# Other row orders for one scratch array, the residual rows and the output rows of a spectral filter with an MLP

## The chip, the cores and the metric

The kernel runs on one core of a Trainium2 chip. The metric is device time in microseconds (us). The time before is 407.89 us, the median of three runs (407.39 to 407.97). The profile is of one execution that took 407.44 us; its span, from the first to the last instruction, is 405.2 us, so 2.24 us lie around it. All times on the trace count from the start of the span.

## The reference

```python
def _A_ref(x, w_r, w_i):
    X = rfft2(x); X = X * (w_r + 1j * w_i)
    return irfft2(X, (S, D))
def _B_ref(x, w1, b1, w2):
    h = x @ w1 + b1
    return (h * tanh(softplus(h))) @ w2          # Mish
xn = _layernorm(A_x)
return A_x + _A_ref(xn, A_w_r, A_w_i) + _B_ref(xn, B_w1, B_b1, B_w2)
```

x has S = 2048 rows of D = 512 floats (4 MB), the MLP's hidden width is F = 1792. The result is the input plus a filter in the two-dimensional frequency domain plus an MLP, both of the normalized input.

## The kernel before, in words

Row number 1024 w + 16 t + 4 g + 2 i + q is written as w (2 halves), t (64), and the residue s2 = 4 g + 2 i + q of 16. The work is in **four groups g** of 512 rows.

**The MLP** runs as 56 tiles (g, f), f one of 14 slices of F, each with two half tiles. `mlp_up` does 12 matmuls `ph` (L735), a Mish on ScalarE (L743) and a split into two half-precision parts (L343 on ScalarE, L344 on VectorE); `mlp_down` does 12 matmuls `pa` (L88 to L92), some tiles later. After the last up tile of a group g < 3, `rows_back` (L778) loads the group's 512 residual rows into `macc[g]`, two transfers of 512 KB. After its last down tile `mlp_end` (L787) adds the MLP's sum to them (L793), and for g = 3 stores each quarter at once, one half from SyncE's queue (SP) and one from ScalarE's.

**The transform** takes four steps out (`s1_forward`, `p2_unit`, `d_pair`, and the product with the weights in `spectrum`) and four back. Between the steps the data is turned through scratch arrays in DRAM: `d_y1`, `d_a`, `d_t`. In `dp_unit` the tile `at` goes to `d_a` (L693); `ip_unit` loads it turned as `ai` (L701), multiplies (`psT`), and its tile `tt` goes to `d_t` (L717). `at`, `tt` and the earlier `y1` share three buffers, so a new one is written once the transfer of the third one before has landed. `spectrum` also moves a few short rows, `g<-es` (L609) and `u<-h` (L665), and uses the former in VectorE's L656. Two tiles `y` (L832) take the residual rows of the last group.

**The last step**, `s1_inverse`, runs eight times, for (g, q) in the order (3,0), (3,1), (0,0), (0,1), (1,0), (1,1), (2,0), (2,1). Each takes two tiles `yi` of 128 partitions (L843), made of two 64-partition halves, one for each of two parities. They come from the two planes of `d_t`, one transfer per half. Twelve matmuls `psY` (L866) follow, then VectorE (L882, L883) and GpSimd (L884) add the result to the residual rows; for g < 3 `store_rows` (L856) then sends 512 KB out in two transfers. In the loop over the eight, a step first loads the `yi` of the next one, then issues the stores of the one before, then multiplies.

**The order.** Loads and stores stand in SP's one instruction stream, in order; an issue that waits holds all behind it. TensorE's order in the last step is that of the program: half tiles of the MLP between the eight steps, as many as a rule with `T_LAG` and `T_HOLD` gives:

```python
while done[0] - start < T_LAG + k * (total - T_HOLD - T_LAG - start) / (n - 1) and half_tile():
    pass
```

With 15 half tiles left and n = 8, they stand 3, 1, 1, 2, 1, 1, 1, 1 ahead of the steps and 4 behind the last one.

Of the kernel before, what the change touches and what calls it, by code (L numbers as in the profile page):

```python
# [11 lines left out]
F16 = mybir.dt.float16  # L12
# [7 lines left out]
P = 128  # L20
NS2 = 16
# [6 lines left out]
E_UP = 11  # L28
N_WGT = 117.6
B_END = 97  # L30
T_LAG = 2.5
T_HOLD = 4


O_P2, O_IP2, O_D, O_ID2, O_ID = 0, 1024, 2048, 4096, 5120
# [4 lines left out]
def spectral_mlp_kernel(ctx, tc, x, wt, w0, w1, b1, w2, cT, cIT, cM, out):  # L40
    nc = tc.nc
# [11 lines left out]
    dp = ctx.enter_context(tc.tile_pool(name="dp", bufs=1, space=bass.MemoryType.DRAM))  # L53
# [1 line left out]
    nc.scalar.preload_act_table_set("mish")  # L55
    xv = x.rearrange("(p s) d -> p s d", s=NS2)

    xp = x.rearrange("(w t s) d -> t w s d", w=2, s=NS2)
    outp = out.rearrange("(w t s) d -> t w s d", w=2, s=NS2)


    d_y1 = dp.tile([64, P, 256], F16, tag="d_y1", name="d_y1")
    d_a = dp.tile([16, 2, P, 2 * 256], F16, tag="d_a", name="d_a")
    d_t = dp.tile([2, 64, 64, 256], F16, tag="d_t", name="d_t")

    @contextmanager
    def in_order(*engines):
# [18 lines left out]
    def mm3(ps, stat, mov, start, stop, order=False):  # L86

        first = nc.tensor.matmul(ps, stat(0), mov(0), start=start, stop=False)  # L88
        if order:
            tc.keep_in_program_order(first)  # L90
        nc.tensor.matmul(ps, stat(0), mov(1), start=False, stop=False)  # L91
        return nc.tensor.matmul(ps, stat(1), mov(0), start=False, stop=stop)  # L92
# [27 lines left out]
    def butterfly(out, a, b, scale, name):  # L120

        bc = tp.tile([P, 256], F32, tag="bc", name=f"bc_{name}", bufs=2)
        nc.scalar.mul(bc, b, scale)
        t = tp.tile([P, 4, 2, 64], F32, tag="bt", name=f"bt_{name}", bufs=2)
        av = a.rearrange("p (k e) -> p k e", k=4)
        bv = bc.rearrange("p (k e) -> p k e", k=4)
        nc.vector.scalar_tensor_tensor(t[:, :, 0], av, scale, bv, op0=ALU.mult, op1=ALU.add)
        last = nc.vector.scalar_tensor_tensor(t[:, :, 1], av, scale, bv, op0=ALU.mult, op1=ALU.subtract)  # L128
        tv = t.rearrange("p k c e -> p k (c e)")
        nc.scalar.copy(out[:, :, 0, :], tv)  # L130
        nc.gpsimd.tensor_sub(out[:, :, 1, :], tv, out[:, :, 0, :])  # L131
        return last.ins
# [565 lines left out]
    def ip_unit(c, g):  # L698
        fg = 4 * c + g
        ai = qp.tile([P, 4, 2, 2, 64], F16, tag="q1", name=f"ai_{fg}")  # L700
        nc.sync.dma_start(ai.rearrange("p (b r) h c e -> p b (r h c e)", b=2), d_a[fg].rearrange("b p e -> p b e"))  # L701
        ps = ps_f.tile([P, 2, 4, 64], F32, tag="f", name=f"psT_{fg}")
        for k in range(2):
            parts = [(1, slice(0, 1)), (0, slice(1, 4))] if fg == 0 else [(0, slice(0, 4))]
            for n, (v, ls) in enumerate(parts):
                mm3(
                    ps[:, k, ls],
                    lambda h: c_ip2[:, k, v, h, :],
                    lambda h: ai[:, ls, h, k, :],
                    True,  # L710
                    True,
                    k == 0 and n == 0,
                )
        tt = tp.tile([P, 4, 2, P], F16, tag="q2", name=f"tt_{fg}", bufs=3)
        butterfly(tt, ps[:, 0].rearrange("p l e -> p (l e)"), ps[:, 1].rearrange("p l e -> p (l e)"), 2.0**-12, f"t_{fg}")
        for be in range(2):
            nc.sync.dma_start(  # L717
                d_t[be].rearrange("a (c f) e -> (a c) (f e)", c=2)[:, fg * 512 : (fg + 1) * 512],
                tt[:, 2 * be : 2 * be + 2].rearrange("p l h e -> p (l h e)"),
            )  # L720


    macc, yacc, last, wait, in_a = {}, {}, {}, [], []
# [54 lines left out]
    def rows_back(g):  # L778

        macc[g] = cp.tile([P, 4, D], F32, tag=f"xnT{g}", name=f"m_{g}")  # L780
        for i in range(2):
            nc.sync.dma_start(
                macc[g][64 * i : 64 * i + 64].rearrange("t (w q) d -> t w q d", w=2),
                xp[:, :, 4 * g + 2 * i : 4 * g + 2 * i + 2],
            )

    def mlp_end(g):  # L787
        if g == 3:
            macc[g] = cp.tile([P, 4, D], F32, tag=f"xnT{g}", name=f"m_{g}")
        m = macc[g]  # L790
        for s in range(4):
            xr = yacc[g][s] if g == 3 else m[:, s, :]
            nc.vector.scalar_tensor_tensor(m[:, s, :], pacc[g][s], sc["out"], xr, op0=ALU.mult, op1=ALU.add)  # L793
            if g == 3:
                for i, eng in enumerate((nc.sync, nc.scalar)):
                    eng.dma_start(outp[:, s // 2, 4 * g + 2 * i + s % 2], m[64 * i : 64 * i + 64, s, :])

    def mlp_all():

        tiles = [(g, f) for g in range(4) for f in range(NFC)]  # L800
        acts = {}
        up = down = n_down = 0
        while down < len(tiles):
            lag = LEAD if sc["ahead"] else LAG

            home = sc["ahead"] and up % 12 > 3
            free = down >= up - up % 4 - 8 if home else len(in_a) < NA or in_a[-NA] < down
            if free and up < len(tiles) and (up < E_UP or up - down < lag or (n_down >= 2 and up - down > lag)):
                mlp_up(*tiles[up], acts)
                if tiles[up][1] == NFC - 1 and tiles[up][0] < 3:  # L810
                    rows_back(tiles[up][0])
                up += 1
                n_down = 0
            else:
                g, f = tiles[down]
                mlp_down(g, f, acts.pop((g, f)))
                if f == NFC - 1:
                    mlp_end(g)
                down += 1
                n_down += 1  # L820
            yield 1
# [6 lines left out]

    def load_y(q):
        y = sc["y", q] = big.tile([P, 2, D], F32, tag="big", name=f"y_{q}")  # L830
        for i in range(2):
            nc.sync.dma_start(y[64 * i : 64 * i + 64], xp[:, :, 12 + 2 * i + q])  # L832

    yi_of, to_store = {}, []

    def load_yi(g, q):

        yis = []
        for i in range(2):
            s2 = 4 * g + 2 * i + q  # L840
            yi = qp.tile([P, 4, 2, P], F16, tag="q1", name=f"yi_{s2}")
            for be in range(2):
                nc.sync.dma_start(  # L843
                    yi[64 * be : 64 * be + 64].rearrange("p a h e -> p a (h e)"),
                    d_t[be, 4 * s2 : 4 * s2 + 4].rearrange("a p e -> p a e"),
                )
            yis.append(yi.rearrange("p a h (b e) -> p h b a e", b=2))
        yi_of[g, q] = yis

    def store_rows():  # L850

        while to_store:
            g, q = to_store.pop(0)
            mv = macc[g].rearrange("p (w q) d -> p w q d", w=2)
            for i in range(2):
                nc.sync.dma_start(outp[:, :, 4 * g + 2 * i + q], mv[64 * i : 64 * i + 64, :, q])  # L856

    def s1_inverse(g, q):

# [32 lines left out]
    def half_tile():  # L892
        if next(B, None) is None:
            return False
        done[0] += 1
        return True
# [12 lines left out]
    def stream_a():  # L909

        todo = []

        def behind(n):
            if len(todo) > n:
                ip_unit(*todo.pop(0))
                yield 1.0

        for c in range(5):
            if c < 4:
                for g in range(0, 4, 2):  # L920
                    p2_unit(c, g)
                    p2_unit(c, g + 1)
                    yield 1.6
                    yield from behind(0)
            if c:
                for g in range(4):
                    dp_unit(c - 1, g)
                    todo.append((c - 1, g))
                    yield 0.8
                    yield from behind(4)  # L930
            if c < 4:
                for wgt in spectrum(c):
                    yield wgt
                    yield from behind(0)
        while todo:
            ip_unit(*todo.pop(0))
            yield 1.0
# [95 lines left out]
    for wgt in stream_a():  # L1033
        used += wgt
        while done[0] - start < used * (B_END - start) / N_WGT and half_tile():
            pass

    load_y(0)
    load_y(1)
    todo = [(3, q) for q in range(2)] + [(g, q) for g in range(3) for q in range(2)]  # L1040
    load_yi(*todo[0])
    start, n = done[0], len(todo)
    total = 2 * 4 * NFC
    with in_order(mybir.EngineType.PE):
        for k in range(n):
            while done[0] - start < T_LAG + k * (total - T_HOLD - T_LAG - start) / (n - 1) and half_tile():
                pass
            if k + 1 < n:
                load_yi(*todo[1])
            store_rows()  # L1050
            s1_inverse(*todo.pop(0))
        store_rows()
        while half_tile():
            pass
# [180 lines left out]
```

## Time and profile before

| | us |
|---|---|
| median of three runs | 407.89 |
| the profiled execution | 407.44 |
| its span | 405.2 |
| TensorE matmul busy | 382.8 (94%) |
| VectorE busy | 256.8 (63%) |
| ScalarE busy | 206.7 (51%) |
| GpSimd busy | 82.3 (20%) |
| DMA, mean of 16 engines | 51.0% on SP's queue |

A timeline row has the start, the length, the engine, the line, the operation, the written and the read tile, the shape and the count; in brackets stands the idle time ahead of it and what ended it. SPq is SP's issuing of transfers: its length is that of the issuing, not of the transfer. In the rows of stretches, the pairs are busy time and count for TensorE, its weight loads, VectorE, ScalarE and GpSimd; then come TensorE's granted clock, the busy share of the 16 DMA engines and the GB/s that they moved. A row on one line's issues has the shortest, the median and the longest in ns.

### The profile page before, as it was taken

How to read it: one execution, taken by the hardware profiler on the slowest of the kernel's cores; microseconds unless marked ns; L12 is line 12 of the kernel's file. 1: busy time of each engine (PE TensorE's matmuls, PEld its weight loads, DVE VectorE, ACT ScalarE, POOL GpSimd, SP SyncE). 2: the span in 40 equal slices, each digit the busy share in tenths (PEclk: the TensorE clock that was granted, in tenths of full speed). 3: DMA queues.
4: the chain of work that ended last, by engine and by line, in shares of the span. 5: the costliest groups of instructions: out<-in, count | busy, mean ns of one | idle time of the engine just before them, and what ended most of it. 6: DMA issues, size and time to landing. Idle time of an engine off the chain costs nothing.

```text
span 405.2 us, 6791 instructions
## 1 busy us (share of the span) xinstructions
PE 382.8 (94%) x2533; PEld 189.3 (47%) x2533; DVE 256.8 (63%) x528; ACT 206.7 (51%) x333; POOL 82.3 (20%) x111
## 2 busy tenths in 40 slices
PE   8999998799998999999999999999998999879994
PEld 3444443345454454555454555445544455424341
DVE  5889768558787169644977439773369933335642
ACT  3879853576553265546465445463455543514220
POOL 0000038566654000000121001210011111313430
PEclk9999999999999999999999999999999999969998
DMA  8995015273287930626827263173831117445764
GB/s 284 366 397 228 2 52 155 79 194 119 77 289 211 274 115 3 161 49 172 220 78 181 80 182 106 42 195 105 208 118 40 59 47 187 139 142 148 199 188 141
DMA packets 52864, 61.10 MB, mean 151 GB/s; under 512 B 4432, under 2 KB 40784, under 8 KB 52704
## 3 DMA queue, kind: packets, MB, share of 16 engines
q1 hardware_dynamic: 52512, 60.15, 51.0%
q10 hardware_dynamic: 320, 0.52, 0.4%
q8 instruction: 20, 0.33, 0.3%
q14 instruction: 12, 0.10, 0.1%
HBM read 43.85 MB, written 16.78 MB: 150 GB/s over the span
## 4 chain that ended last, share of the span: by engine, by line
PE 54%; DVE 16%; ACT 8%; issue 8%; POOL 7%; DMA 3%; SPq 3%; POOLq 0%; DVEq 0%; ACTq 0%
PE ph L735 19%; PE pa L88 7%; PE pa L92 7%; PE pa L91 7%; PE psD L553 3%; PE ps_warm L216 3%; PE psP L529 2%; POOL y L131 2%; ACT a L343 2%; ACT hb L743 2%; DVE st L178 2%; SPq L843 2%; DVE m L793 1%; POOL xh L196 1%; DVE a L344 1%
## 5 line engine op out<-in xcount | busy, mean ns | idle before, releaser
L735 PE MATMUL ph<-xnT,w1t 128*128 128x512 f16 x672 | 154.3, 379 | 1.9 <-ACT xnT L300 1.0
L735 PEld LDWEIGHTS <-w1t 128*128 128x128 f16 x672 | 64.2, 98 | 79.8 <-issue 3.8
L88 PE MATMUL pa<-w2r,a 128*128 128x512 f16 x224 | 85.1, 383 | 3.2 <-DVE m L793 2.9
L91 PE MATMUL pa<-w2r,a 128*128 128x512 f16 x224 | 85.6, 382 | 0.8 <-DVE w2r L344 0.7
L92 PE MATMUL pa<-w2r,a 128*128 128x512 f16 x224 | 85.4, 381 | 0.0
L344 DVE SCALAR_TENSOR_TENSOR a<-hb,sc_a,a 128x512 f16<-128x512 f32 x56 | 42.8, 767 | 60.2 <-ACT a L343 59.8
L743 ACT ACTIVATE hb<-ph,b1t,sc_exp 128x512 f32<-128x512 f32 x56 | 43.3, 773 | 49.5 <-PE ph L735 49.4
L131 POOL TENSOR_TENSOR tt<-bt_t,tt 128x512 f16<-128x512 f32 x16 | 19.3, 1209 | 195.8 <-ACT tt L130 195.8
L343 ACT ACTIVATE a<-hb,sc_a 128x512 f16<-128x512 f32 x56 | 40.1, 720 | 1.5
L91 PEld LDWEIGHTS <-a 128*128 128x128 f16 x224 | 22.0, 98 | 27.8 <-issue 4.6
L88 PEld LDWEIGHTS <-a 128*128 128x128 f16 x224 | 22.0, 98 | 27.8 <-issue 4.1
L92 PEld LDWEIGHTS <-a 128*128 128x128 f16 x224 | 22.1, 98 | 27.6 <-issue 2.2
L131 POOL TENSOR_TENSOR y<-bt_s,y 128x512 f16<-128x512 f32 x16 | 20.1, 1262 | 18.1 <-ACT y L130 18.1
L343 ACT ACTIVATE u<-r,sc_u 128x512 f16<-128x512 f32 x16 | 11.5, 718 | 22.0 <-DVE r L633 14.9
L130 ACT CAST y<-bt_s 128x512 f16<-128x512 f32 x16 | 9.9, 617 | 14.7 <-DVE bt_s L128 8.1
L130 ACT CAST tt<-bt_t 128x512 f16<-128x512 f32 x16 | 9.9, 618 | 14.1 <-DVE bt_t L128 10.8
L542 DVE SCALAR_TENSOR_TENSOR z<-psP,z 128x512 f16<-128x512 f32 x16 | 10.6, 686 | 9.3 <-ACT z L541 9.3
L565 ACT ACTIVATE ix<-psD 64x512 f32<-64x512 f32 x16 | 9.5, 594 | 13.6 <-PE psD L553 13.4
L688 DVE SCALAR_TENSOR_TENSOR at<-psA,at 128x512 f16<-128x512 f32 x16 | 10.7, 687 | 8.9 <-ACT at L687 8.9
L196 POOL TENSOR_TENSOR xh<-xs,xh 128x512 f16<-128x512 f32 x12 | 14.4, 1217 | 4.0 <-ACT xh L195 4.0
L216 PE MATMUL ps_warm<-warm 128*128 128x512 f16 x47 | 13.9, 455 | 1.2 <-DVE warm L211 1.2
L687 ACT ACTIVATE at<-psA 128x512 f16<-128x512 f32 x16 | 9.1, 589 | 10.7 <-issue 8.0
(147 smaller groups left out, 521.5 us busy)
## 6 DMA issues: line engine op xcount, KB each, us to landing
wt<-in_wt_dram SPq DMA_DIRECT2D x32, 256.0 KB
x<-in_x_dram SPq DMA_DIRECT2D x8, 512.0 KB
d_y<-y SPq DMA_DIRECT2D x16, 256.0 KB
wm<-in_wt_dram SPq DMA_DIRECT2D x8, 512.0 KB
yt<-d_y SPq DMA_DIRECT2D x16, 256.0 KB
d_a<-at SPq DMA_DIRECT2D x32, 128.0 KB
ai<-d_a SPq DMA_DIRECT2D x16, 256.0 KB
d_t<-tt SPq DMA_DIRECT2D x32, 128.0 KB
```

The source lines that it names most:

```text
L88: first = nc.tensor.matmul(ps, stat(0), mov(0), start=start, stop=False)
L91: nc.tensor.matmul(ps, stat(0), mov(1), start=False, stop=False)
L92: return nc.tensor.matmul(ps, stat(1), mov(0), start=False, stop=stop)
L130: nc.scalar.copy(out[:, :, 0, :], tv)
L131: nc.gpsimd.tensor_sub(out[:, :, 1, :], tv, out[:, :, 0, :])
L196: nc.gpsimd.tensor_sub(xh[:, 1, :], xs, xh[:, 0, :])
L216: nc.tensor.matmul(ps, warm[:, 0:P], warm, start=True, stop=True)
L343: hi = nc.scalar.activation(dst_h, src, AF.Copy, scale=scale)
L344: lo = nc.vector.scalar_tensor_tensor(dst_l, src, scale, dst_h, op0=ALU.mult, op1=ALU.subtract)
L553: first = nc.tensor.matmul(ps[be][:, k], c_d[rows, k0 + k, e, hs, :], z[rows, hm, 2 * (k0 + k) + e].rearrange("p g q -> p (g q)"), start=e ...
L735: last_mm = nc.tensor.matmul(ph, w1t[:, hs, dc, f * P : (f + 1) * P], xnT[g][:, hm, dc, :], start=n == 0, stop=n == 11)
L743: nc.scalar.activation(hb, ph, AF.Mish, bias=b1t[:, f : f + 1], scale=s_exp[k])
```

## The change

1. `d_t` becomes one plane `[64, 128, 256]`; the middle index is (parity, c, f). The stores of `tt` (now L718) write rows of 1 KB to a destination walked as (a 64, c 2). A `yi` tile comes by one transfer of 128 partitions, [128, 4, 256], in place of two of 64 (now L842): 16 transfers in place of 32.
2. The residual loads go by w in place of i. Each fills all 128 partitions, partition p = 64 i + t, from a DRAM view walked as (i 2, t 64): `rows_back` (now L783) with rows of 4 KB, `load_y` (L832) with rows of 2 KB. Bytes and counts of transfers stay.
3. The stores go by w as well: a destination walked as (i 2, t 64) with rows of 2 KB, from 128 partitions (now L854, 12 of 256 KB as before). The last group's quarters go in one 256 KB store each, from SP (L796), in place of two of 128 KB from SP and ScalarE.
4. `T_LAG` 3 and `T_HOLD` 3: the 15 half tiles stand 3, 2, 1, 1, 2, 1, 1, 1 ahead of the steps and 3 behind.

```diff
-T_LAG = 2.5
-T_HOLD = 4
+T_LAG = 3
+T_HOLD = 3
...
-    xp = x.rearrange("(w t s) d -> t w s d", w=2, s=NS2)
-    outp = out.rearrange("(w t s) d -> t w s d", w=2, s=NS2)
+    xp = x.rearrange("(w t g i q) d -> w g i t q d", w=2, t=64, g=4, i=2, q=2)
+    outp = out.rearrange("(w t g i q) d -> w g q i t d", w=2, t=64, g=4, i=2, q=2)
...
-    d_t = dp.tile([2, 64, 64, 256], F16, tag="d_t", name="d_t")
+    d_t = dp.tile([64, P, 256], F16, tag="d_t", name="d_t")
...
+        rows = d_t.rearrange("a (b c f) e -> b a c (f e)", b=2, c=2)
         for be in range(2):
             nc.sync.dma_start(
-                d_t[be].rearrange("a (c f) e -> (a c) (f e)", c=2)[:, fg * 512 : (fg + 1) * 512],
+                rows[be, :, :, fg * 512 : (fg + 1) * 512],
                 tt[:, 2 * be : 2 * be + 2].rearrange("p l h e -> p (l h e)"),
             )
...
-        for i in range(2):
+        for w in range(2):
             nc.sync.dma_start(
-                macc[g][64 * i : 64 * i + 64].rearrange("t (w q) d -> t w q d", w=2),
-                xp[:, :, 4 * g + 2 * i : 4 * g + 2 * i + 2],
+                macc[g][:, 2 * w : 2 * w + 2].rearrange("p q d -> p (q d)"),
+                xp[w, g].rearrange("i t q d -> i t (q d)"),
             )
...
             if g == 3:
-                for i, eng in enumerate((nc.sync, nc.scalar)):
-                    eng.dma_start(outp[:, s // 2, 4 * g + 2 * i + s % 2], m[64 * i : 64 * i + 64, s, :])
+                nc.sync.dma_start(outp[s // 2, g, s % 2], m[:, s, :])
...
-        for i in range(2):
-            nc.sync.dma_start(y[64 * i : 64 * i + 64], xp[:, :, 12 + 2 * i + q])
+        for w in range(2):
+            nc.sync.dma_start(y[:, w], xp[w, 3, :, :, q])
...
-            for be in range(2):
-                nc.sync.dma_start(
-                    yi[64 * be : 64 * be + 64].rearrange("p a h e -> p a (h e)"),
-                    d_t[be, 4 * s2 : 4 * s2 + 4].rearrange("a p e -> p a e"),
-                )
+            nc.sync.dma_start(
+                yi.rearrange("p a h e -> p a (h e)"),
+                d_t[4 * s2 : 4 * s2 + 4].rearrange("a p e -> p a e"),
+            )
...
-            mv = macc[g].rearrange("p (w q) d -> p w q d", w=2)
-            for i in range(2):
-                nc.sync.dma_start(outp[:, :, 4 * g + 2 * i + q], mv[64 * i : 64 * i + 64, :, q])
+            for w in range(2):
+                nc.sync.dma_start(outp[w, g, q], macc[g][:, 2 * w + q])
```

The scheduler moves some instructions. On SP, in the last step, the rows before were these; the shape is that of what is written, `out_dram` the result, and the number of `m_` tells the group (931 is g = 0, 2294 is 1, 3453 is 2, the last one 3).

```order
L856 DMA out_dram<-m_931 64x2x512 x2
L843 DMA yi_4394<-d_t 64x4x256 x2
L843 DMA yi_4397<-d_t 64x4x256 x2
L856 DMA out_dram<-m_931 64x2x512 x2
L843 DMA yi_4440<-d_t 64x4x256 x2
L843 DMA yi_4443<-d_t 64x4x256 x2
L856 DMA out_dram<-m_2294 64x2x512 x2
L843 DMA yi_4480<-d_t 64x4x256 x2
L843 DMA yi_4483<-d_t 64x4x256 x2
L856 DMA out_dram<-m_2294 64x2x512 x2
L856 DMA out_dram<-m_3453 64x2x512 x4
L796 DMA out_dram<-m_4598 64x512 x4
```

On SP, the same place of the changed program:

```order
L854 DMA out_dram<-m_931 2x64x512 x2
L842 DMA yi_4402<-d_t 128x4x256
L842 DMA yi_4404<-d_t 128x4x256
L854 DMA out_dram<-m_931 2x64x512 x2
L842 DMA yi_4440<-d_t 128x4x256
L842 DMA yi_4442<-d_t 128x4x256
L854 DMA out_dram<-m_2294 2x64x512 x2
L842 DMA yi_4484<-d_t 128x4x256
L842 DMA yi_4486<-d_t 128x4x256
L854 DMA out_dram<-m_2294 2x64x512 x2
L854 DMA out_dram<-m_3453 2x64x512 x4
L796 DMA out_dram<-m_4582 2x64x512 x4
```

The order stays; the `yi` transfers are half as many, and the outermost count of the stores' destination is 2 where it was 64.

On VectorE, in the second of the four runs of `spectrum` (c = 1), the use of the short rows `g_1` (L656) moves ahead, as the difference shows:

```order
 L572 TENSOR_TENSOR t_a_1_2408<-xa_1_2402,wt_1_1_1946 128x256
+L656 TENSOR_TENSOR r_1_2595<-g_1_2229,c0t 4x4x32
 L573 TENSOR_TENSOR ra_1_2407<-ra_1_2407,t_a_1_2408 128x256
+L657 TENSOR_TENSOR m_1_0_2596<-g_1_2229,c0t 4x128
 L631 TENSOR_TENSOR r_1_2266<-ra_1_2407 128x4x32
```

L656 stood eight instructions further on, behind L128; now the product L573, two splits and the eviction of `psT` (L127, L128) stand behind it.

On SP, ahead of the fourth run of `spectrum` (c = 3), the changed program has these rows, with the residual load of g = 2 at the head:

```order
L783 DMA m_3453<-in_x_dram 128x1x1024 x2
L693 DMA d_a<-at_3469 64x4x256 x2
L693 DMA d_a<-at_3487 64x4x256 x2
L693 DMA d_a<-at_3517 64x4x256 x2
L693 DMA d_a<-at_3535 64x4x256 x2
L701 DMA ai_3618<-d_a 128x2x512
L701 DMA ai_3702<-d_a 128x2x512
```

Before, the first `ai` stood ahead of the two transfers of `at_3535`; now it stands behind them.

## The prediction

> **What bounds the kernel now.** I read the page first, then the stretches, then the waits of the last 60 us.
>
> ```profile
> span 405.2 us, 6791 instructions
> ```
>
> ```profile
> 16.00:24.00 8.00, 7.91 (x43) 3.65 (x43) 6.75 (x11) 5.74 (x9) 0.38 (x1) 1.00 1.05 387
> 134.00:344.00 210.00, 206.55 (x1595) 109.37 (x1594) 130.05 (x283) 107.03 (x176) 16.17 (x14) 1.00 0.46 123
> 353.50:361.50 8.00, 4.87 (x19) 1.73 (x20) 2.76 (x4) 1.94 (x3) 1.06 (x1) 0.62 0.58 170
> 366.00:371.00 5.00, 5.00 (x33) 2.04 (x31) 2.83 (x5) 2.08 (x3) 2.38 (x2) 1.00 0.55 161
> ```
>
> TensorE is the bound: from 134 to 344 it works 206.55 of 210 us, in an order that nothing can rearrange while the kernel runs. So whatever makes it wait there is added to the time in full. Its one weak place is the end, where it waits for turned rows:
>
> ```profile
> PE psY L866 <- DMA yi<-d_t: 4.7, 4, 2.9
> ```
>
> That is four waits, 4.7 us in all, the longest 2.9 at the first `psY`; after it the granted clock averages 0.62 over eight us.
>
> **The transfers that the change touches,** by their issues on SP:
>
> ```profile
> 82.19 0.77 SPq L782 DMA_DIRECT2D m<-in_x_dram  x1
> ...
> 193.66 1.36 SPq L782 DMA_DIRECT2D m<-in_x_dram  x2
> ...
> 197.35 1.34 SPq L609 DMA_DIRECT2D g<-es  x2
> ...
> 275.40 1.31 SPq L832 DMA_DIRECT2D y<-in_x_dram  x2
> 283.34 1.29 SPq L782 DMA_DIRECT2D m<-in_x_dram  x2
> 286.30 4.28 SPq L693 DMA_DIRECT2D d_a<-at  x6
> 291.30 0.38 SPq L701 DMA_DIRECT2D ai<-d_a  x1
> ```
>
> ```profile
> 344.10 7.37 SPq L717 DMA_DIRECT2D d_t<-tt  x8
> 352.52 17.53 SPq L843 DMA_DIRECT2D yi<-d_t  x20
> 371.44 1.92 SPq L856 DMA_DIRECT2D out_dram<-m  x2
> ...
> 398.85 2.49 SPq L796 DMA_DIRECT2D out_dram<-m  x4
> ```
>
> **What the reshaping asks of the DMA engines.** The new residual loads and all new stores have one side walked as (2, 64, row), the other as 128 partitions. The question that decides everything is over how many of the 16 engines such a transfer spreads. The page's packet counts tell it for the shapes of before:
>
> ```profile
> DMA packets 52864, 61.10 MB, mean 151 GB/s; under 512 B 4432, under 2 KB 40784, under 8 KB 52704
> ...
> q10 hardware_dynamic: 320, 0.52, 0.4%
> ```
>
> ```profile
> wt<-in_wt_dram SPq DMA_DIRECT2D x32, 256.0 KB
> ...
> g<-es SPq DMA_DIRECT2D x16, 1.0 KB
> u<-h SPq DMA_DIRECT2D x16, 1.0 KB
> w0t<-in_w_dram SPq DMA_DIRECT2D x4, 8.0 KB
> cMt<-in_cM_dram SPq DMA_DIRECT2D x1, 32.0 KB
> b1t<-in_b_dram SPq DMA_DIRECT2D x1, 7.0 KB
> ```
>
> Queue 10 carries four stores of 64 rows: 256 data packets, and 64 more, 16 for each store. I read these as one closing packet per engine. The whole list of issues (23 groups, its first and last above) has 280 transfers. Data rows under 512 B are 64 in `g`, 64 in `u`, 128 in `cMt`, 128 in `b1t`, together 384; so 4432 - 384 = 4048 closing packets. Were it 16 for each transfer, there would be 4480. The 432 that are missing are 12 for each of 36 transfers, and just 36 have an outermost count of 4 (`g` 16, `u` 16, `w0t` 4). So 64 or 128 in front gives 16 engines, 4 gives 4. In all of these a small outermost count is also a small number of rows, so the trace leaves open whether the 128 rows of (2, 64) count as 2 or as 128. What the generator works from shows in its issue times:
>
> ```profile
> L701 SPq DMA_DIRECT2D ai<-d_a x16: 360/376/563, 184.3 to 342.7; - x16
> ```
>
> ```profile
> L508 SPq DMA_DIRECT2D wt<-in_wt_dram x32: 471/547/588, 122.7 to 267.7; - x32
> ```
>
> ```profile
> L843 SPq DMA_DIRECT2D yi<-d_t x32: 573/615/1030, 352.5 to 385.8; - x32
> ```
>
> `ai` has 256 rows behind an outermost 128 and costs 376 ns, `wt` 64 rows behind a 64 and costs 547: the outermost count, not the rows, goes with the cost. I take it that the split over engines goes by the outermost count too, so that (2, 64) runs on **two engines**, the same two each time.
>
> The Trainium skill, page "DMA: Bandwidth & Descriptors", section "Why a DMA increments its semaphore by 16 and not by 1", gives this as a rule against the change: the engines used are the largest number up to 16 that divides the slowest count above 1 of both sides, and on this path they are the lowest-numbered ones. The trace agrees for 4, 64 and 128; no run here shows a 2. By the rule the time is the sum below; by the other reading of the packet counts it is the first rival's.
>
> **Part by part, on two engines.** In the fastest stretch 16 busy engines moved 387 GB/s, 24.2 each. A 256 KB transfer (131,072 bytes on each of two) then takes 5.42 us, one of 512 KB 10.8. Each engine works its packets off in order, so what is issued behind on SP waits for these two even if the other 14 are free.
>
> *Loads of `m`, g = 0.* Issued at 82.2, they hold two engines to about 105; only prefetches and the slack buffers of `y1` lie behind. 0 us taken, up to 4 possible.
>
> *Loads of `m`, g = 1.* Two transfers, 21.7 us. The second half of the short rows `g` is issued behind them, and L656, which reads it, now stands ahead of L573:
>
> ```profile
> 199.30 0.42 DVE L573 TENSOR_TENSOR ra<-ra,t_a 128x256 f32<-128x256 f32 x1
> ...
> 202.89 0.28 DVE L656 TENSOR_TENSOR r<-g,c0t 4x128 f32<-4x128 f32 x1
> ```
>
> ```profile
> 208.32 1.48 PE L553 MATMUL psD<-z,cMt 64*128 64x256 f16 x24
> ```
>
> ```profile
> 337.40 2.65 DMA ai<-d_a
> ```
>
> A small transfer lands 2.65 us after its issue, so I put about 1.2 ahead of the bytes and 1.2 behind. `g` lands at 193.66 + 1.2 + 21.7 + 1.2 = 217.8, and VectorE stands from 199.3 to there, 18.5 us. Behind it is the eviction of two `psT`, whose buffers `psD` needs; VectorE is done with them 0.7 us ahead of 208.32 now. **17.8 us** on TensorE; the bound below is 0, if the load did not delay `g`.
>
> *Loads of `y` and of `m`, g = 2.* `y` is 10.8 us, `m` 21.7: from 276.6 the two engines are taken to 309.1. The `d_a` issued at 286.3 land behind, at 310.3 or so. Eight `d_a` now stand ahead of the first `ai`, so this is issued at about 310.8 and lands at 313.4. TensorE wants it here:
>
> ```profile
> 297.83 0.27 PE L88 MATMUL psT<-ai,cMt 128*128 128x256 f16 x1
> ```
>
> **15.6 us**; below, again 0. The second `y` has 10.8 us at 321.5 with nothing urgent behind it: 0.
>
> *Clock after the two stalls.* After the 2.9 us wait in the last step, 4.87 us of matmul work ran at 0.62, which is 1.9 us lost. Twice: **3.8 us**, 0 to 6.
>
> *The last step.* The `yi` cost less: a pair of steps' tiles by two issues of 376 ns in place of four of 615 is 1.7 us earlier at the first `psY`, less about 0.5 because `d_t`'s new destination has a 64 in front (eight issues, partly behind other waits): **-1.2**. Then the stores: 16 of 256 KB, each 5.42 us on the same two engines, 86.7 us. Six `yi` (steps (1,1), (2,0), (2,1)) stand between them; in the stretch from 366 to 371 an engine moved 161 / (16 x 0.55) = 18.3 GB/s while busy, so 16 KB each is 0.9 us, 5.4 together. From the first store's issue to the span's end that is 92.1, and about 4.0 for the start of the first and the end of the last (3.9 lie behind the last issue at 401.3 now): 96.1. It is 405.2 - 371.4 = 33.8 now. **+62.3**. TensorE's waits for the late `yi` and its last three half tiles lie under these stores: (2,1) can start at about 412 less the shift, and the stores run to about 464. That the quarters of g = 3 leave in one store each, and that three rather than four half tiles follow the last step, costs nothing, for the queue is full then.
>
> Sum: 407.4 + 17.8 + 15.6 + 3.8 - 1.2 + 62.3 = 505.7, **506 us**. The profiled execution lies 0.45 under the median of the runs, which is nothing here.
>
> **The rivals.**
>
> 1. *All 16 engines serve (2, 64).* For it: 128 rows are there to be shared, and each packet count of before fits that too. Against it: the issue costs go by the outermost count. Then only the `yi` count: -1.2 at the first wait, and the other three waits (4.7 - 2.9 = 1.8), which come from issues crowded on SP, mostly go; about -2.4 with the last stores' issue unchanged to 0.1. 405.0 us, the other side. It holds from 16 engines down to about eight, where a store takes 1.4 us.
> 2. *Two engines, but the loads up front are covered,* by the MLP's lag of tiles: only the last step counts, 407.4 + 61.1 = 468.5 us. Against it: the in-order waits named above.
> 3. *Two engines, but not the same two each time.* Then transfers overlap, nothing queues, and only the last store's own 5.42 us shows, some 4 us more than rival 1: 409 us. No row speaks for or against it.
>
> **How the numbers follow.** The forecast has 0.76, rival 1 0.11, rival 2 0.08, rival 3 0.05. If the rate of two engines is a tenth lower, the terms of transfer grow by about 13, and small waits may add some: the upper end is 526. The lower end is 466, just under rival 2. What is left out is rivals 1 and 3, 0.16, and a few hundredths. A measurement of this kernel can tell about 0.2% (0.8 us). Faster is rival 1, 0.10 without its edge; same 0.02; slower 0.88.
>
> **What would show it.** In the profile of the changed kernel: 2 closing packets per reshaped transfer, so fewer packets under 512 B; a DMA share near 2/16 over the last 60 to 80 us, with some 48 GB/s; idle VectorE ahead of L656 at c = 1, idle TensorE ahead of `psT` and `psD`; `psY` of the last three steps spaced by about 12 us. I am wrong if the stores of one step land 3 us after their issue, or if TensorE waits for nothing before 344.

## The result: 512.9 us, a quarter slower

The changed kernel takes **512.86 us** (median of six runs, 511.19 to 513.54) against 407.96 (six runs, 407.39 to 408.68) for the kernel before: a ratio of **1.2565**, interval 1.254 to 1.2589. The forecast was 506, its range 466 to 526. The profiled execution took 513.39 us.

The page of the changed kernel has the span, the busy time of the engines, the DMA share in tenths and the GB/s by fortieths of the span, and the packets:

```profile
span 511.5 us, 6760 instructions
...
PE 396.5 (78%) x2533; PEld 193.1 (38%) x2533; DVE 254.9 (50%) x528; ACT 206.8 (40%) x333; POOL 81.9 (16%) x111
...
DMA  9980242337790435203634261241116622221111
GB/s 295 378 336 2 61 144 75 107 129 247 201 267 11 109 78 150 105 35 98 171 89 133 69 169 49 78 127 54 48 56 186 185 84 81 86 86 52 51 51 45
DMA packets 52180, 61.10 MB, mean 119 GB/s; under 512 B 3748, under 2 KB 40100, under 8 KB 52020
```

The DMA row of before:

```profile
DMA  8995015273287930626827263173831117445764
```

The bytes are the same, 61.10 MB. The last four slices (51 us) run at about 50 GB/s with a DMA share of one tenth, where before had four to seven tenths at its end: a few engines work and the others have nothing. The packets say how few. There are 260 transfers now, 16 `yi` and four stores fewer. Taking off the 384 short data packets, 3748 - 384 = 3364 closing ones are left, and 198 x 16 + 36 x 4 + **26 x 2** = 3364 exactly, 26 being the six loads of `m`, four of `y` and 16 stores.

Where the time went can be read from the same issues in both kernels, since those named below stand at one place in SP's list. Three of before that the prediction did not show:

```profile
129.26 3.06 SPq L508 DMA_DIRECT2D wt<-in_wt_dram  x5
...
232.95 4.75 SPq L693 DMA_DIRECT2D d_a<-at  x6
...
334.11 2.63 SPq L693 DMA_DIRECT2D d_a<-at  x4
```

The same ones, and those between them that the change touches, in the changed kernel:

```profile
85.15 2.86 SPq L783 DMA_DIRECT2D m<-in_x_dram  x1
...
137.27 3.07 SPq L508 DMA_DIRECT2D wt<-in_wt_dram  x5
...
202.88 8.29 SPq L609 DMA_DIRECT2D g<-es  x2
...
261.25 4.75 SPq L693 DMA_DIRECT2D d_a<-at  x6
...
311.65 2.78 SPq L783 DMA_DIRECT2D m<-in_x_dram  x2
314.60 27.20 SPq L693 DMA_DIRECT2D d_a<-at  x8
...
382.47 2.62 SPq L693 DMA_DIRECT2D d_a<-at  x4
...
420.89 1.21 SPq L854 DMA_DIRECT2D out_dram<-m  x2
...
476.63 20.09 SPq L796 DMA_DIRECT2D out_dram<-m  x4
```

The differences of these starts, each less the one before it, split the whole 511.5 - 405.2 = 106.3 us:

| stretch | predicted | measured |
|---|---|---|
| up to 129.26 (loads of `m`, g = 0) | 0 (up to 4) | 8.0, of which 0.7 arise in the first 10 us of the span |
| to 232.95 (`m`, g = 1; with its clock) | 17.8 + 1.9 | 20.3 |
| to 334.11 (`y`, `m`, g = 2; with its clock) | 15.6 + 1.9 | 20.1 |
| to the first store's issue | -1.2 | 1.1 |
| first store's issue to the end | 62.3 | 56.8 |

Who waits, from the waits of the changed kernel (engine, tile and line, what ended the wait: us in all, times, longest):

```profile
ACT at L687 <- DMA d_a<-at: 23.3, 2, 22.3
PE psD L553 <- DVE at L688: 20.9, 1, 20.9
PE psY L864 <- DMA yi<-d_t: 20.5, 8, 5.9
...
DVE r L656 <- DMA g<-es: 18.0, 1, 18.0
...
PE psD L553 <- DVE bt_t L128: 17.5, 2, 14.4
ACT y L130 <- DMA d_y<-y: 7.5, 1, 7.5
```

At g = 1 VectorE stands 18.0 us ahead of L656, and TensorE's `psD` 17.5 us, in two waits, for the eviction behind it. At g = 2 ScalarE waits 22.3 us for a buffer `at` that a `d_a` transfer has not left, and `psD` 20.9 us for a PSUM buffer that L688, behind that `at`, has still to read. In the last step all eight `psY` wait for `yi`. Stretches of the changed kernel (columns as before):

```profile
229.00:237.00 8.00, 3.09 (x25) 1.80 (x26) 4.50 (x12) 4.31 (x7) 2.31 (x2) 0.50 0.14 46
237.00:245.00 8.00, 8.00 (x37) 3.72 (x37) 6.64 (x12) 4.63 (x8) 0.00 (x0) 0.86 0.63 171
340.50:343.00 2.50, 2.41 (x23) 1.87 (x22) 0.79 (x2) 0.72 (x1) 0.00 (x0) 0.50 0.37 89
343.00:351.00 8.00, 8.00 (x38) 3.67 (x36) 6.09 (x17) 4.87 (x9) 1.22 (x1) 0.88 0.44 139
476.00:506.00 30.00, 0.00 (x0) 0.00 (x0) 0.00 (x0) 0.00 (x0) 0.00 (x0) 0.50 0.13 51
```

After each stall the granted clock starts at 0.50 and averages 0.86 and 0.88 over the following eight us. From 476 to 506 nothing computes; 51 GB/s leave on 0.13 x 16 = 2.1 engines.

### The profile page after: what moved, and what is told of

The parts are those of the page before. It is cut to its first block, busy times and chain, and to the rows that moved or that the text cites. A ratio compares the mean times of both kernels' runs of the same rounds, so it can differ in the third digit from the quotient of the medians.

```text
span 511.5 us, 6760 instructions
## 1 busy us (share of the span) xinstructions
PE 396.5 (78%) x2533; PEld 193.1 (38%) x2533; DVE 254.9 (50%) x528; ACT 206.8 (40%) x333; POOL 81.9 (16%) x111
## 2 busy tenths in 40 slices
DMA packets 52180, 61.10 MB, mean 119 GB/s; under 512 B 3748, under 2 KB 40100, under 8 KB 52020
## 4 chain that ended last, share of the span: by engine, by line
PE 44%; DMA 18%; DVE 11%; ACT 7%; issue 5%; POOL 4%; SPq 2%; DVEq 0%; POOLq 0%; ACTq 0%
PE ph L736 15%; DMA yi<-d_t 7%; PE pa L88 7%; PE pa L91 7%; PE pa L92 6%; DMA d_a<-at 3%; PE psD L553 3%; DMA g<-es 3%; DMA d_y<-y 2%; ACT a L343 2%; ACT hb L744 2%; PE psP L529 2%; DMA w1s<-in_w_dram 1%; DVE st L178 1%; SPq L693 1%
## 5 line engine op out<-in xcount | busy, mean ns | idle before, releaser
L91 PE MATMUL pa<-w2r,a 128*128 128x512 f16 x224 | 88.3, 394 | 0.8 <-DVE w2r L344 0.7
L88 PE MATMUL pa<-w2r,a 128*128 128x512 f16 x224 | 88.0, 396 | 0.3 <-ACT w2r L343 0.3
L92 PE MATMUL pa<-w2r,a 128*128 128x512 f16 x224 | 87.5, 391 | 0.0
L553 PE MATMUL psD<-z,cMt 64*128 64x256 f16 x192 | 15.9, 305 | 38.5 <-DVE at L688 20.9
L88 PEld LDWEIGHTS <-a 128*128 128x128 f16 x224 | 22.6, 101 | 30.7 <-issue 8.5
L92 PEld LDWEIGHTS <-a 128*128 128x128 f16 x224 | 22.7, 101 | 29.4 <-issue 5.5
L91 PEld LDWEIGHTS <-a 128*128 128x128 f16 x224 | 22.5, 101 | 25.8 <-issue 3.8
L343 ACT ACTIVATE u<-r,sc_u 128x512 f16<-128x512 f32 x16 | 11.5, 718 | 40.2 <-DVE r L633 32.3
L553 PEld LDWEIGHTS <-cMt 64*128 64x128 f16 x192 | 10.5, 105 | 44.9 <-issue 23.6
L864 PE MATMUL psY<-yi,cITt 64*64 64x512 f16 x96 | 11.0, 475 | 20.5 <-DMA yi<-d_t 20.5
L688 DVE SCALAR_TENSOR_TENSOR at<-psA,at 128x512 f16<-128x512 f32 x16 | 10.7, 687 | 31.1 <-ACT at L687 31.1
L880 DVE SCALAR_TENSOR_TENSOR m<-psY,sc_k,m 128x512 f32<-128x512 f32 x12 | 8.7, 747 | 31.8 <-PE psY L864 31.8
L131 POOL TENSOR_TENSOR y<-bt_s,y 128x512 f16<-128x512 f32 x16 | 20.1, 1261 | 25.4 <-ACT y L130 25.4
L130 ACT CAST y<-bt_s 128x512 f16<-128x512 f32 x16 | 9.9, 617 | 20.9 <-DMA d_y<-y 7.5
L873 ACT ACTIVATE odd<-psY,sc_k 128x512 f32<-128x512 f32 x8 | 5.4, 680 | 31.5 <-PE psY L864 20.5
```

The source lines that it names most:

```text
L343: hi = nc.scalar.activation(dst_h, src, AF.Copy, scale=scale)
L553: first = nc.tensor.matmul(ps[be][:, k], c_d[rows, k0 + k, e, hs, :], z[rows, hm, 2 * (k0 + k) + e].rearrange("p g q -> p (g q)"), start=e ...
L688: nc.vector.scalar_tensor_tensor(at[:, :, 1, :], psv, 2.0**-15, at[:, :, 0, :], op0=ALU.mult, op1=ALU.subtract)
L864: mm = nc.tensor.matmul(ps[be][64 * i : 64 * i + 64].rearrange("p (b a e) -> p b a e", b=2, a=4), sc["cIT"][rows, 4 * g + 2 * i + q, hs, : ...
```

## The experiments

Theory A is that of the prediction: the outermost count of 2 confines each reshaped transfer to the same two DMA engines, and what needs these engines waits. The rivals put the loss on the moved instructions, on rows by w, on `d_t`, or on SP's one queue.

### Only the walk (`e_k64`): (t 64, i 2) in place of (i 2, t 64)

```diff
-    xp = x.rearrange("(w t g i q) d -> w g i t q d", ...)
-    outp = out.rearrange("(w t g i q) d -> w g q i t d", ...)
+    xp = x.rearrange("(w t g i q) d -> w g t i q d", ...)
+    outp = out.rearrange("(w t g i q) d -> w g q t i d", ...)
...
-                xp[w, g].rearrange("i t q d -> i t (q d)"),
+                xp[w, g].rearrange("t i q d -> t i (q d)"),
```

> The changed kernel with one thing else: residual loads and all stores walk the DRAM rows as (t 64, i 2) in place of (i 2, t 64). Same bytes, same rows, same 128 partitions, same count of transfers, same order of instructions on every engine; only the outermost count is 64 in place of 2. (Within each transfer the rows are dealt to other partitions, so a row of the output mixes residual and result of two rows.) Theory A, the outermost count of 2 confines each of these transfers to two DMA engines: all of the loss is gone, 405 us (403 to 408), packets under 512 B up by 36 x 14 - 12 (14 x 26 = 364 more closing packets), no wait of VectorE ahead of L656 at c = 1. Rival B, the cost lies in the new order of instructions (L656 ahead, eight d_a ahead of the first ai) or in rows by w: the loss stays for the most part, above 480 us. Rival C, part of each: the loads' 47 us stay because L656 stands early, the stores' 57 go: about 455 us.

Measured: **401.8 us**, ratio 0.9861 (0.9843 to 0.988). In this kernel and the next three the rows of the result do not keep their places; they serve for the time alone. The page, and L656 with three issues named above:

```profile
span 399.8 us, 6760 instructions
...
DMA packets 52544, 61.10 MB, mean 153 GB/s; under 512 B 4112, under 2 KB 40464, under 8 KB 52384
```

```profile
199.76 0.28 DVE L656 TENSOR_TENSOR r<-g,c0t 4x128 f32<-4x128 f32 x1 [0.78 <-DMA g<-es]
...
233.43 4.92 SPq L693 DMA_DIRECT2D d_a<-at  x6
...
332.59 2.61 SPq L693 DMA_DIRECT2D d_a<-at  x4
...
370.89 1.22 SPq L854 DMA_DIRECT2D out_dram<-m  x2
```

There are 364 packets more than in the changed kernel, 14 for each of 26 transfers (the expectation's "36 x 14 - 12" is a slip for this). By the traces, the instructions of every engine stand in the same order as in the changed kernel. All of the loss is gone with nothing changed but the outermost count, so B and C fall: the moved instructions cost 0.78 us at L656. The time is 3 us under the 405 expected and below the range. From 232.95 and 334.11 before to 233.43 and 332.59 here, the stretch of g = 2 is 2.0 us shorter.

### The dose (`e_k4`, `e_k8`, `e_k16`): outermost counts 4, 8 and 16

```diff
+    xp = x.rearrange("(w t i g q) d -> w g i t q d", w=2, i=K, g=4, q=2)
+    outp = out.rearrange("(w t i g q) d -> w g q i t d", w=2, i=K, g=4, q=2)
```

> The changed kernel with the DRAM rows of residual loads and stores walked as (i 4, t 32); everything else, the order of instructions on every engine too, is as in the changed kernel (which rows make up a transfer changes, so the output's rows are dealt otherwise). Theory A, four engines: 65,536 bytes on each at the 26.1 GB/s that the last stores of the changed kernel showed are 2.51 us a store; 16 of them, 5 us for yi and 4 for start and end make 49 us where it was 33.8 before, +15; g = 1: 10 us of loads ahead of g in place of 20, so VectorE waits 6 to 8 us there; g = 2: 1 to 5 us; g = 0: 1 to 2 us. About 432 us (424 to 442); 12 closing packets fewer per transfer than with 16 engines. Rival D, the engines are two whatever the outermost count below 16 or so: about 512 us. Rival E, any count above two already spreads over all 16: 405 us.

> The same with (i 8, t 16). Theory A, eight engines: 1.25 us a store, all under TensorE's last step save about 1 at the end; 5 us of loads ahead of g, which leave 0 to 3 us of VectorE's wait. 408 us (404 to 413). Rival D: about 512 us.

> The changed kernel with the rows walked as (i 16, t 8). If the count of engines is the outermost count up to 16, this is as good as e_k64: 402 us (401 to 404), 52,544 packets. If more than 16 are needed, by the series 2, 4, 8 (the loss halving each time, 21 us at 8): 412 us.

| outermost count | us | packets under 512 B | closing per transfer | L656 waits | first store to end |
|---|---|---|---|---|---|
| 2 (the change) | 512.86 | 3748 | 2 | 18.0 | 90.6 |
| 4 | 446.96 | 3800 | 4 | 11.1 | 51.2 |
| 8 | 425.30 | 3904 | 8 | 6.8 | 37.8 |
| 16 | 407.19 | 4112 | 16 | 1.8 (for `yt`) | 30.4 |
| 64 (above) | 401.80 | 4112 | 16 | 0.8 | 28.9 |

The ratios to before are 1.0958 (1.0943 to 1.0974), 1.0424 (1.0404 to 1.0444) and 0.9995 (0.9972 to 1.0018). The count of closing packets is the outermost count up to 16, exactly, each worked out as above; D and E fall. By the traces, these three kernels too keep the order of the changed kernel on every engine. From 4 to 2 the stores' stretch grows by 39.4 us, and 16 stores of 5.02 in place of 2.51 would be 40.2. The Trainium skill's rule (page "DMA: Bandwidth & Descriptors", section "Why a DMA increments its semaphore by 16 and not by 1"), the largest number up to 16 that divides the slowest counts, agrees at all five. Every count here divides 16 or is a multiple of it, so no run tells dividing from a cap at 16.

My sizes were off for 4 and 8: 432 and 408 expected, 447 and 425 measured, both outside their ranges. I had given each engine 26 GB/s whatever their number. For 16 the 407 lie between the two theories, 402 and 412: the closing packets are those of the first, the time is not. Stretches while the loads for g = 1 and the last stores run, count 4:

```profile
204.00:208.00 4.00, 4.00 (x23) 2.00 (x21) 0.00 (x0) 0.00 (x0) 0.00 (x0) 1.00 0.26 103
...
433.00:441.00 8.00, 0.00 (x0) 0.00 (x0) 0.00 (x0) 0.00 (x0) 0.00 (x0) 0.50 0.26 102
```

and count 8:

```profile
200.00:204.00 4.00, 4.00 (x20) 1.84 (x19) 0.00 (x0) 0.00 (x0) 0.00 (x0) 1.00 0.69 137
...
414.00:420.00 6.00, 0.00 (x0) 0.00 (x0) 0.06 (x1) 0.00 (x0) 0.00 (x0) 0.70 0.50 162
```

Four engines move 103 / (16 x 0.26) = 24.8 GB/s each in the loads and 24.5 in the stores. With eight it is 20.3 in the stores; in the loads the 137 / (16 x 0.69) = 12.4 is no rate of the eight, for 16 x 0.69 = 11 engines were busy, so other transfers are in it. Why an engine is slower in the stores with eight, and why a count of 16 is 5 us behind 64 with as many closing packets, stays open: these kernels also space the rows of a transfer differently (64, 128 and 256 KB apart along t with counts 4, 8 and 16; 32 KB with 64). The Trainium skill, same page, section "Latency and other measured facts", gives copies 207 GB/s at a row pitch of 512 KiB and 164 at 2 MiB. No run here has such a pitch or changes the spacing alone.

### The loads alone, the stores alone

Each is the kernel before with the diff's lines for the residual loads, or for the stores.

> The kernel before with one part of the change: residual loads (m and y) by w, walked (i 2, t 64). Stores, d_t, yi and the lag stay as before. Theory A, two engines and what queues behind: the shifts that the changed kernel showed up to its last step, 7.3 + 20.3 + 20.1 = 47.7 us, less what k = 64 shows the moved order to be worth by itself (2 to 4 us): 452 us (446 to 458). Rival B, the loads cost only together with the new d_t or the lag: below 430 us.

> The kernel before with the other part alone: stores by w, walked (i 2, t 64), the last quarters in one store each from SP. Loads, d_t, yi and the lag stay as before. Theory A: 16 stores of 5.02 us on two engines, 80.3, plus six pairs of yi halves at about 0.9 and 4 for start and end, so 90 us from the first store's issue to the end of the span where it was 33.8: 407.4 + 56 = 464 us (458 to 470); with the loads' part it adds up to the whole. Rival B, the stores cost only because the loads had emptied TensorE's lead first: below 450 us.

Measured: 455.32 us, ratio 1.1165 (1.1146 to 1.1185), for the loads, and 463.49, ratio 1.1368 (1.1343 to 1.1393), for the stores. Waits of the first:

```profile
ACT at L687 <- DMA d_a<-at: 23.9, 2, 22.9
PE psD L553 <- DVE at L688: 21.5, 1, 21.5
...
DVE r L656 <- DMA g<-es: 18.7, 1, 18.7
...
ACT y L130 <- DMA d_y<-y: 7.1, 1, 7.1
```

First and last stores of the second, whose span is 461.3 us:

```profile
370.27 1.68 SPq L854 DMA_DIRECT2D out_dram<-m  x2
...
426.38 20.09 SPq L795 DMA_DIRECT2D out_dram<-m  x4
```

The loads alone bring every wait of the changed kernel ahead of its last step. The stores alone need 461.3 - 370.3 = 91.0 us from first issue to end, 90.6 in the changed kernel. The two add up: 47.6 + 55.7 = 103.3 of the 104.9 us. The parts are independent to within 1.6 us, and both B fall.

### The same stores from two queues

```diff
-                nc.sync.dma_start(outp[s // 2, g, s % 2], m[:, s, :])
+                (nc.scalar if s // 2 else nc.sync).dma_start(outp[s // 2, g, s % 2], m[:, s, :])
...
-            for w in range(2):
-                nc.sync.dma_start(outp[w, g, q], macc[g][:, 2 * w + q])
+            for w, eng in enumerate((nc.sync, nc.scalar)):
+                eng.dma_start(outp[w, g, q], macc[g][:, 2 * w + q])
```

> The changed kernel with half of the stores (w = 1, and the last two quarters) issued from ScalarE's queue in place of SP's; the transfers themselves stay as they are. Theory A, the two engines' bytes are the bound: a second queue adds no engine, the stores take 16 x 5.02 us as before, 512 us (505 to 517); SP's issues are stretched less. Rival Q, the bound is the one queue working its transfers off in turn, or SP's blocked issue: with two queues the stores overlap, some 40 us less, about 470 us.

Measured: 511.88 us, ratio 1.2553 (1.2522 to 1.2584). First and last of SP's half:

```profile
417.27 0.60 SPq L854 DMA_DIRECT2D out_dram<-m  x1
...
470.36 17.21 SPq L796 DMA_DIRECT2D out_dram<-m  x2
```

The span is 508.0 us, so the stretch is 508.0 - 417.3 = 90.7 us, as with one queue. Rival Q falls: the engines are the bound. SP's last two issues take 8.6 us each in place of 5.0, which fits that each now waits for stores of the other queue too.

### The same loads from ScalarE's queue

In `rows_back` and `load_y`, `nc.sync` becomes `nc.scalar`.

> The changed kernel with the residual loads (m and y) issued from ScalarE's queue in place of SP's; the transfers stay on two engines, the stores as they are. Theory A1, g and d_a wait because they stand behind the loads in the same queue, and SP's issue is held: with another queue, the waits ahead of L656 at c = 1 and ahead of at in g = 2 fall from 18.0 and 22.3 to under 6 us each; 475 us (465 to 490). Theory A2, the two engines take what comes first from any queue and are full for 20 us each time: the waits stay above 12 us each, 500 to 513 us.

Measured: 489.63 us, ratio 1.2007 (1.1948 to 1.2065).

```profile
ACT at L687 <- DMA d_a<-at: 5.9, 2, 5.0
...
DVE r L656 <- DMA g<-es: 3.6, 1, 3.6
```

Both waits fall to what A1 said, so most of these two came from standing behind the loads in one queue; A2 falls. The queue is not all that changed: the scheduler moved instructions too (L573 stands ahead of L656 again, and one `ai` ahead of the last two `d_a`). But `g` was issued by 198.7 and in use at 205.2, where the changed kernel issued it by 211.2 and used it at 225.2.

The time is at the upper end of A1's range: by the same issues the shifts are 3.0, 7.3 and 15.5 us in place of 8.0, 20.3 and 20.1. At g = 2 SP issues one `ai` and then stands still for eleven us ahead of the last `d_a`, with three `ai` behind it:

```profile
310.57 0.38 SPq L701 DMA_DIRECT2D ai<-d_a  x1
322.15 1.24 SPq L693 DMA_DIRECT2D d_a<-at  x2
323.49 2.19 SPq L701 DMA_DIRECT2D ai<-d_a  x3
```

```profile
SPq L693 <- DMA m<-in_x_dram: 11.1, 1, 11.1
```

The tile `at` had been ready since 311.2. By the trace, what ended SP's wait was the landing of a load `m` from the other queue; with the waits at other lines put down to a load `m` or `y`, SP stood 25 us in all. Why an issue on SP waits for a load on ScalarE's queue is not shown. So a second queue takes `g` out from behind the loads and still leaves SP bound to them.

The Trainium skill, page "DMA: Bandwidth & Descriptors", section "Queues, rings and completion order", says that an engine takes packets from its queues in turn. That agrees: `g` no longer stands behind the loads, but from its issue to its use it takes 6.5 us, where `e_k64` needs 3.2.

### What the other parts are worth

`e_halves` is the changed kernel with loads and stores by i; the next two are the kernel before with `d_t` and `yi`, and with the lag. The last takes `e_halves` and issues the load of g = 2 one half tile later:

```diff
+                if tiles[up][0] == 3 and tiles[up][1] == 1:
+                    rows_back(2)
-                if tiles[up][1] == NFC - 1 and tiles[up][0] < 3:
+                if tiles[up][1] == NFC - 1 and tiles[up][0] < 2:
                     rows_back(tiles[up][0])
```

> The changed kernel with residual loads and all stores by the halves i as before; the new scratch layout of d_t, the one-transfer yi and the lag of three stay. Theory A: 405 us (403 to 408), since only the reshaped transfers cost, and the yi of one transfer save a little at the first psY. Rival B, the d_t writes with a destination of (64, 2) or the 128-partition yi are at fault: above 480 us.

> The kernel before with the new d_t and the yi of one transfer alone (loads, stores and lag as before). My prediction put this at -1.2 us at the first psY, and about 1 us more at the later ones: 405 to 407 us. Rival: d_t's issues, now 613 ns in place of 405, give back what yi's save, 407 to 408.5 us, no difference.

> The kernel before with T_LAG 3 and T_HOLD 3 alone. A theory in which one more half tile ahead of the second step covers the late yi: 406 to 407 us, with the waits of psY for yi below 4.7 us. A rival in which the end after the last step has one half tile less to cover the stores: 408 to 409 us. If neither: 407.5 to 408.

> The kernel e_halves (loads and stores by the halves, new d_t and lag) with the residual load of g = 2 issued one half tile later in the program, which lets the scheduler put eight d_a ahead of the first ai and a TensorE order close to that of the changed kernel. e_k64 was 4 us faster than e_halves with the orders of the changed kernel. If that gain is the order's (theory O): 402 us (401 to 404). If it is that 128-partition transfers by w are cheaper than halves (theory W): 405 to 406 us, as e_halves.

| kernel | us | ratio (interval) |
|---|---|---|
| `e_halves` | 405.81 | 0.9949 (0.9931 to 0.9966) |
| `e_dt` | 405.91 | 0.9959 (0.9942 to 0.9977) |
| `e_lag` | 406.17 | 0.9974 (0.9958 to 0.999) |
| `e_late` | **404.01** | 0.9907 (0.9889 to 0.9925) |

The `d_t` layout and `yi` are a gain of 0.4%, about 1.7 us, and the lag one of 0.3%, about 1.1; both intervals end just below 1. Their rivals fall. With the lag alone the waits for `yi` go from 4.7 to 4.4 us only, so where the rest of its gain lies is not shown. The waits for `yi` with `d_t` alone, against 4.7 us in four with the longest 2.9 before:

```profile
PE psY L866 <- DMA yi<-d_t: 4.0, 2, 3.6
```

The first wait is longer, 3.6 us, and of the three later ones one is left, of 0.4. `e_late`, with nothing on two engines, beats both kernels, and is the fastest here that leaves every row in its place. It lies between theories O and W. Its order on TensorE is still not quite that of `e_k64`, so how the 4 us between `e_halves` and `e_k64` split between order and transfer shape stays open.

## Why the prediction was right, point by point

- **Two engines: right,** and shown twice over, by the count of closing packets and by the run that changes the outermost count alone. The inference from before rested on counts of 4 and on issue times, and only the first of these held (the list that it counts has 24 groups, not 23; the 280 transfers are right). The issue times do not go by the outermost count. The first row is the stores of the changed kernel, with a count of 2, the second those of `e_k64`:

```profile
L854 SPq DMA_DIRECT2D out_dram<-m x12: 559/2738/7081, 420.9 to 471.6; - x12
...
L854 SPq DMA_DIRECT2D out_dram<-m x12: 539/554/1274, 370.9 to 391.4; - x12
```

The shortest issue takes 559 ns with 2 and 539 with 64; with 4, 8 and 16 it is 536, 598 and 539. So by the traces of before alone, taking (2, 64) as 2 and not as 128 was a choice that came out right.

- **Rival 1 (16 engines), 405.0:** its premise was false. Given 16 engines the kernel takes 401.8 (count 64) or 407.2 (count 16), around its number. That it would hold down to about eight engines is wrong: eight took 425.3.
- **Rival 2 (the loads are covered), 468.5:** the stores alone measure 463.5, so that sum was good; its premise fell with the loads' 47.6 us.
- **Rival 3 (not the same pair):** the 16 stores would have overlapped. They take 5.02 us each, one after the other. The last three steps' `psY` start at 434.98, 446.78 and 458.57, the 12 us apart that the prediction named as a sign.
- **`m`, g = 0, priced at 0: wrong, about 7 us.** The step said that only prefetches and slack buffers lie behind. ScalarE's `y` waited 7.5 us for a buffer whose `d_y` transfer needed the two busy engines. The slack was shorter than the 21 us, and the bound of 4 too low.
- **`m`, g = 1:** 17.8 us for TensorE's wait against 17.5 in the rows, at the place named. The moved L656 was the right link.
- **`y` and `m`, g = 2:** 15.6 against 20.9. The place was wrong: not `psT` for its `ai`, but `psD`, one step up, for the buffer `at`. I followed what the loaded data feed and not who waits for a buffer that an outgoing transfer still holds.
- **Clock, 3.8:** by the rows above 3.09 x 0.50 + 8.00 x 0.14 = 2.7 us after the first stall and 2.41 x 0.50 + 8.00 x 0.12 = 2.2 after the second, 4.8 in all before rounding. So at g = 1 the 20.3 are 17.5 of waiting and 2.7 of clock. At g = 2, 20.9 and 2.2 would be 23.1, and 20.1 were measured. `e_k64`, with the same order and without the stall, is 2.0 shorter there than before, a gain that no term of mine held; 1.0 stays open.
- **First `psY`, -1.2: wrong in sign.** Its wait was 3.35 us against 2.9, and with `d_t` and `yi` alone it was 3.6, so fewer issues did not bring the tile earlier. The first store's issue came 1.1 later: one more half tile stands ahead of the second step, which I had not counted (with the lag alone that issue goes from 371.4 to 373.8).
- **Stores, +62.3 against +56.8:** the mechanism was right and the rate off. A store took 5.02 us and not 5.42, since 131,072 bytes per engine passed at 26.1 GB/s and not 24.2. Over 16 stores that is 6.4 us, the whole miss and a little more.

In spans the sum is 8.0 us low (106.3 against 98.3): by the table the first four stretches are 8.0, 0.6, 2.6 and 2.3 too small and the last 5.5 too large. That the total came out near is partly this offsetting.

## What to carry to other kernels

Before reshaping a transfer, look at the outermost count on both sides, DRAM's too: 128 partitions on one side did not help where the other was walked as (2, 64), and two engines carried what sixteen had carried. Closing packets (here one per engine and transfer, among those under 512 B) tell from the page, once the short data rows are taken off, over how many engines the transfers spread. When a few engines are held, price every transfer that is issued behind, by who waits for its buffer as well as who waits for its data.

## What the runs showed that I had not expected

- **SP's issue itself is held.** An issue of `d_a` normally takes 608 ns, one of `g` 616; behind the two-engine loads they took up to 9.68 and 7.63 us, and the last stores 4.95 each, the pace of the stores. So SP is held at its issue of transfers that need nothing from the loads' data.

```profile
L693 SPq DMA_DIRECT2D d_a<-at x32: 574/608/9684, 189.0 to 388.5; - x32
```

```profile
L796 SPq DMA_DIRECT2D out_dram<-m x4: 4947/4949/4950, 476.6 to 491.8; - x4
```

- **The rate of one engine is not fixed:** 26.1 GB/s in stores on two engines, 24.5 on four, 20.3 on eight.
- **A residual load's shape moved the compute order.** With the loads by w the scheduler set eight `d_a` ahead of the first `ai`. The fastest run has that order with full transfers. One late load brought the eight `d_a` back in `e_late`, and 1.8 of the 4.0 us between `e_halves` and `e_k64`.
